# Attention by tiles of 128 tokens, with scores as 64x64 products in the quarters of the array

## The chip, the cores and the metric

The kernel runs on one core of a Trainium2 chip. Its engines are PE (TensorE, matrix products), DVE (VectorE), ACT (ScalarE), POOL (GpSimd) and SP (SyncE, which issues most DMAs). The metric is the time of one execution in device microseconds.

## The reference

Sliding-window attention (4 batches, 8 heads, 576 positions, 64 wide, window 64), whose rows then go through a mixture of 8 experts and a dense two-layer network:

```python
scores = scale * np.matmul(q, k.transpose(0, 1, 3, 2))       # (4, 8, 576, 576), d = 64
mask = (rel >= 0) & (rel < 64)
attn = softmax(np.where(mask, scores, -1e9))
x = (attn @ v).transpose(0, 2, 1, 3).reshape(2304, 512)
...
logits = normed(x) @ normed(expert_emb).T / tau               # one of 8 experts for each token
out[mask] = gate_w[mask, None] * (np.maximum(x[mask] @ w1[e], 0) @ w2[e])
...
h = np.maximum(x @ w_in, 0);  out = (s * h * h + b) @ w_out
```

## The kernel before

The work has three parts: attention with routing, the experts, the dense network. All products are in float32 accuracy. The change is in attention and in the routing of its rows.

A unit is one pair of heads of one batch (16 units); its head pair `hp` puts head `hp` on partitions 0 to 63 and head `hp + 4` on 64 to 127. `prep` (L219) turns a unit's k and q by PE transposes, in four pieces of three transposes and two evictions each. k goes to `kT`, and q into `qbd`, which holds each window of 64 queries as a 128x128 block whose two off-diagonal quarters are zero, cleared once by memsets (`clear`, L179). A batch has nine windows of 64 queries; a window looks at 128 keys.

A step is three windows of one unit, and there are 48 steps in the order of `steps` (L825). In `scores` (L245) one product per window multiplies the block of `qbd` by 128 columns of `kT`: its output has head h's queries in half h of the partitions. It goes to `sp`, one of two buffers in PSUM. DVE then scales, masks and takes the row minimum of the negated scores (L256, one reduction per 128x128 block), POOL subtracts the minimum (L259, steps 2 to 41), ACT takes the exponential (`exps`, L263). `flip` (L272) transposes the blocks on PE and ACT evicts them as `pT`. `pv` (L280) multiplies by v with a column of ones, in half-array products of 64 output rows, into one of two halves of the bank `pob`; DVE normalises into `xs` (L289 to L291). In `xs` partition halves are heads, so a row of the tile is half a token.

When the four units of a window group are through, `fin` (L678) writes `xs` to `x_dram` in two DMAs, sums squares on POOL (`squares`, L399) or with the turn, and plans the routing with `later`: `route_turn` (L376) transposes a window of x, `route_logits` (L393) multiplies it by the expert embeddings (64 output rows, 8 columns), then come rank, count, list, norm and gate for a batch. `route_norm` (L468) adds the two halves' sums of squares with small products against `fold`. The batch that ends at tile `TF` picks the expert that goes first: `first_weights` (L737) loads its weights, which ACT and POOL split in two parts each (`split`, L86).

PE and SP keep the order in which the loop at L875 to L897 issues: pieces of `prep`, scores of step n, flips of step n - lag, what `later` has for step n, then `pv` of step n - lag - 1. The lag is 2 up to step 41 and 1 after it (L845). `prepare` (L869) runs `prep` ahead by `AHEAD` and `RATE`. k and q of the unit after next and v of the next unit are loaded when a unit is prepared (L833 to L836). The other engines are ordered by the planner's priorities.

Of the kernel before, what the change touches and what calls it, by code (L numbers as in the profile page):

```python
# [20 lines left out]
def tile_kernel(ctx, tc, q, k, v, emb, tau, w1, w2, w_in, w_out, s_in, b_in, out, x_dram, y_dram, y0_dram, wi_dram, wo_dram):  # L21
# [15 lines left out]
    TL = 15  # L37
# [113 lines left out]
    npo = [0]  # L151

    def half_bank(n):
        npo[0] += 1
        return pob[:, npo[0] % 2, :n]

# [18 lines left out]
    qbd = [at.tile([128, NW, 2, 64], F32, name=f"qbd{i}") for i in range(NB)]  # L175
# [10 lines left out]
    G = 3  # L186
    PVP = 20
    NG = NW // G
# [15 lines left out]
    mask = at.tile([128, 2, 128], F32, name="mask")  # L204
    nc.gpsimd.memset(mask, 0.0)
    for h in range(2):
        m = mask[64 * h:64 * h + 64]
        nc.gpsimd.affine_select(out=m[:, 0], in_=m[:, 0], compare_op=ALU.is_ge, fill=-8.0e9,
                                base=-1, pattern=[[1, 128]], channel_multiplier=-1)
        nc.gpsimd.affine_select(out=m[:, 0], in_=m[:, 0], compare_op=ALU.is_ge, fill=-8.0e9,  # L210
                                base=64, pattern=[[-1, 128]], channel_multiplier=1)
        nc.gpsimd.affine_select(out=m[:, 1], in_=m[:, 1], compare_op=ALU.is_ge, fill=-8.0e9,
                                base=0, pattern=[[-1, 128]], channel_multiplier=1)

    xs = {}

    ready = {}

    def prep(b, hp):  # L219

        kt, qt = qk.pop((b, hp))
        qd = qbd[(b * NP + hp) % NB]
        kT = kTs[(b * NP + hp) % NB]
        for nm, src in (("k", kt), ("q", qt)):
            for h in range(2):
# [3 lines left out]
                rows = slice(64 * h, 64 * h + 64)  # L229
                for par in range(2):  # L230
                    if nm == "k":
                        o = kT[rows].rearrange("r (c p e) -> r e c p", c=QC, e=2)[:, par]
                        i = pt[64 * par:64 * par + 64]
                    else:
                        o = qd[rows, :, h].rearrange("r (c w) (p e) -> r e c w p", c=QC, e=2)[:, par]
                        i = pt[64 * par:64 * par + 64].rearrange("r c (w p) -> r c w p", p=32)
# [4 lines left out]
                if nm == "q" and h == 1:  # L241
                    ready[b, hp] = qd, kT
                yield

    def scores(b, hp, g):  # L245
        qd, kT = ready[b, hp]
        sp = ps2.tile([128, G, 128], F32, tag="sp", name="sp")
        for i in range(G):
            w = g * G + i
            k0 = max(w - 1, 0) * 64  # L250
            nc.tensor.matmul(sp[:, i], qd[:, w].rearrange("r h c -> r (h c)"), kT[:, k0:k0 + 128], start=True, stop=True)
        sm = at3.tile([128, G, 128], F32, tag="sm", name="sm")
        mn = at3.tile([128, G], F32, tag="mn", name="mn")
        for i in range(G):
            w = g * G + i
            nc.vector.tensor_tensor_reduce(out=sm[:, i], in0=sp[:, i], in1=mask[:, 1 if w == 0 else 0], scale=-1.0 / 8.0,  # L256
                                           scalar=BIG, op0=ALU.add, op1=ALU.min, accum_out=mn[:, i:i + 1])
        if P0 <= now[0] < PS:
            nc.gpsimd.tensor_tensor(sm, sm, mn.unsqueeze(2).to_broadcast([128, G, 128]), op=ALU.subtract)  # L259
            return sm, None  # L260
        return sm, mn

    def exps(sm, mn):  # L263
        pe = at3.tile([128, G, 128], F32, tag="pe", name="pe")
# [3 lines left out]
        for i in range(G):  # L268
            nc.scalar.activation(pe[:, i], sm[:, i], AF.Exp, bias=mn[:, i:i + 1], scale=-1.0)
        return pe  # L270

    def flip(pe):  # L272
        pt = ps1.tile([128, G, 128], F32, tag="pt", name="pt")
        for i in range(G):
            nc.tensor.transpose(pt[:, i], pe[:, i], ident)
        pT = at3.tile([128, G, 128], F32, tag="pT", name="pT")
# [3 lines left out]
    def pv(b, hp, g, pT):  # L280
        po = half_bank(G * (D + 1)).rearrange("p (i d) -> p i d", i=G)
        for i in range(G):
            w = g * G + i
            for h in range(2):
                rows = slice(64 * h, 64 * h + 64)
                nc.tensor.matmul(po[rows, i], pT[:, i, rows], vbufs[(b * NP + hp) % NB][:, vslot(w), h], start=True, stop=True)
        with tc.high_priority(offset=PVP):
            rc = at3.tile([128, G], F32, tag="rc", name="rc")
            nc.vector.tensor_scalar(rc, po[:, :, D], 1e-9, None, op0=ALU.add)  # L289
            nc.vector.reciprocal(rc, rc)  # L290
            nc.vector.tensor_tensor(xs[b][g][:, :, hp], po[:, :, :D], rc.unsqueeze(2).to_broadcast([128, G, D]), op=ALU.mult)  # L291
# [15 lines left out]
    fold = rp.tile([128, 64], F32, name="fold")  # L307
# [370 lines left out]
    def fin(b, hp, g, pT):  # L678
        pv(b, hp, g, pT)
        if hp < NP - 1:  # L680
            return
# [612 lines left out]
```

## Time and profile before

| | us |
|---|---|
| median of 3 runs | 838.13 |
| lowest, highest | 835.36, 838.35 |
| the profiled execution | 838.74 |
| its span | 837.0 |
| PE busy | 800.7 (96%) |
| DVE busy | 525.3 (63%) |
| ACT busy | 391.8 (47%) |
| POOL busy | 250.2 (30%) |

The span is from the first to the last instruction of the profiled execution. A row of busy time gives the union of an engine's instructions; a matmul's end is modelled, so the start-to-start distance in the timeline tells its price and its own length does not. "[0.33 <-DVE xs L291]" behind a row means that the engine stood still for 0.33 us before it and was released by that instruction. Scores start at 8.84 us, the last are at 148.63, and the experts run alone from about 203 us.

### The profile page before, as it was taken

To read this page: it belongs to the slowest core of one execution; us is meant where nothing else is said; L and a number is where in the kernel's file an instruction comes from. 1 tells how busy PE (TensorE), PEld (TensorE's weight loads), DVE (VectorE), ACT (ScalarE), POOL (GpSimd) and SP (SyncE) were. 2 spreads that over 40 slices of the span, in tenths; PEclk is the share of its full clock that TensorE was granted. 3 is DMA by queue.
4 is the path that set the end of the run, shared out by engine and by line. 5 is a ranking of instruction groups with operands and counts; after the bars stand their busy time and mean duration, and the time that the engine had idled before them with its cause. 6 is when DMAs were issued, how large, how long until landed. Compare 5 with 4: busy or idle time off the path is not lost.

```text
span 837.0 us, 16214 instructions
## 1 busy us (share of the span) xinstructions
PE 800.7 (96%) x6078; PEld 741.3 (89%) x6078; DVE 525.3 (63%) x1358; ACT 391.8 (47%) x813; POOL 250.2 (30%) x281
## 2 busy tenths in 40 slices
PE   7999986898999999899899999999999999999996
PEld 6888875798999999899899999999999999999885
DVE  5757987686877668699565555666655444444442
ACT  6968656414534545446354444444535333332331
POOL 7477765260113352444202222222210010101110
PEclk9999998889999999999999999999999999999999
DMA  9988636245749778687463233333324110100000
GB/s 202 216 205 194 137 81 186 94 139 174 245 149 322 232 248 272 210 267 260 163 217 114 101 101 101 107 117 104 115 89 126 52 45 33 51 26 26 26 26 25
DMA packets 103168, 117.12 MB, mean 140 GB/s; under 512 B 39108, under 2 KB 76996, under 8 KB 103088
## 3 DMA queue, kind: packets, MB, share of 16 engines
q1 hardware_dynamic: 93600, 99.11, 40.5%
q0 software_dynamic: 3232, 10.24, 3.5%
q10 hardware_dynamic: 6256, 6.72, 2.4%
q8 instruction: 48, 0.79, 0.4%
q14 instruction: 32, 0.26, 0.1%
HBM read 91.52 MB, written 24.53 MB: 139 GB/s over the span
## 4 chain that ended last, share of the span: by engine, by line
PE 50%; issue 0%; DMA 0%; POOLq 0%; DVE 0%
PE p L126 49%; PE tp L132 1%; DMA out_dram<-o,ids 0%; POOLq L1289 0%; DVE o L1239 0%; POOLq L1240 0%
## 5 line engine op out<-in xcount | busy, mean ns | idle before, releaser
L126 PE MATMUL p<-xl,wh 128*128 128x256 f32 x576 | 162.4, 282 | 0.0
L126 PE MATMUL p<-xh,wh 128*128 128x256 f32 x576 | 162.2, 282 | 0.0
L126 PE MATMUL p<-xh,wl 128*128 128x256 f32 x576 | 161.8, 281 | 0.0
L1201 ACT ACTIVATE r<-p 128x256 f32<-128x256 f32 x144 | 55.2, 384 | 169.6 <-PE p L126 166.2
L1202 DVE SCALAR_TENSOR_TENSOR r<-r,s_bc 128x256 f32<-128x256 f32 x144 | 82.5, 575 | 80.0 <-ACT r L1201 79.7
L1025 POOL TENSOR_TENSOR fl<-fl,fs 128x512 f32<-128x512 f32 x32 | 45.7, 1430 | 251.8 <-DVE fs L1024 218.3
L126 PE MATMUL p<-wh,gh 128*128 128x512 f32 x288 | 113.0, 392 | 0.0
L126 PE MATMUL p<-wl,gh 128*128 128x512 f32 x288 | 113.0, 392 | 0.0
L126 PE MATMUL p<-wh,gl 128*128 128x512 f32 x288 | 113.0, 392 | 0.0
L126 PEld LDWEIGHTS p<-xh,wh 128*128 128x128 f32 x576 | 108.8, 189 | 0.7
L126 PEld LDWEIGHTS p<-xl,wh 128*128 128x128 f32 x576 | 108.6, 189 | 0.8
L126 PEld LDWEIGHTS p<-xh,wl 128*128 128x128 f32 x576 | 109.0, 189 | 0.0
L88 DVE TENSOR_TENSOR wl<-raw,wh 128x1024 fp32r<-128x1024 f32 x72 | 102.4, 1429 | 6.5 <-ACT wh L87 6.3
L87 ACT ACTIVATE wh<-raw 128x1024 fp32r<-128x1024 f32 x80 | 83.3, 1056 | 4.9 <-DMA raw<-wo_dram 2.1
L1240 POOL DMA_INDIRECT out_dram<-o,ids x18 | 18.7, 1040 | 203.8 <-DVE o L1239 183.3
L126 PE MATMUL p<-hh,wh 128*128 128x256 f32 (+5 forms) x256 | 78.7, 307 | 0.0
L126 PE MATMUL p<-hl,wh 128*128 128x256 f32 (+5 forms) x256 | 77.0, 301 | 0.0
L126 PE MATMUL p<-hh,wl 128*128 128x256 f32 (+5 forms) x256 | 76.9, 300 | 0.0
L1208 ACT ACTIVATE gh<-r,b_bc 128x256 fp32r<-128x256 f32 x144 | 72.5, 503 | 6.1 <-DVE r L1202 5.9
L1209 DVE SCALAR_TENSOR_TENSOR gl<-r,b_bc,gh 128x256 fp32r<-128x256 f32 x144 | 69.1, 480 | 3.1 <-ACT gh L1208 3.1
L126 PEld LDWEIGHTS p<-wh,gl 128*128 128x128 f32 x288 | 54.1, 188 | 12.2
L126 PEld LDWEIGHTS p<-wh,gh 128*128 128x128 f32 x288 | 54.1, 188 | 11.4
(240 smaller groups left out, 1595.4 us busy)
## 6 DMA issues: line engine op xcount, KB each, us to landing
raw<-in_moe_w_dram SPq DMA_DIRECT2D x64, 512.0 KB, 4.8
raw<-y_dram SPq DMA_DIRECT2D x18, 512.0 KB, 3.8
vb<-in_v_dram SPq DMA_DIRECT2D x64, 128.0 KB, 3.8
fr<-in_moe_w_in_dram SPq DMA_DIRECT2D x16, 512.0 KB, 5.1
fr<-in_moe_w_out_dram SPq DMA_DIRECT2D x16, 512.0 KB, 4.4
k<-in_k_dram SPq DMA_DIRECT2D x32, 144.0 KB, 4.0
q<-in_q_dram SPq DMA_DIRECT2D x32, 144.0 KB, 3.8
x_dram<-xs SPq DMA_DIRECT2D x24, 192.0 KB, 3.0
```

The costliest lines, as they stand in the source:

```text
L87: a = nc.scalar.activation(hi, src, AF.Copy)
L88: return a.ins, le.tensor_tensor(lo, src, hi.bitcast(F32), op=ALU.subtract).ins
L126: nc.tensor.matmul(ps, a[x], b[y], start=first and j == 0, stop=last and j == 2)
L132: nc.tensor.matmul(ps, x, y, start=j == 0, stop=j == len(k) - 1)
L1025: nc.gpsimd.tensor_tensor(lf, lf, sg.bitcast(F32), op=ALU.mult)
L1201: nc.scalar.activation(r, ps, AF.Relu)
L1202: nc.vector.scalar_tensor_tensor(r, r, s_bc, r, op0=ALU.mult, op1=ALU.mult)
L1208: nc.scalar.activation(gh, r, AF.Identity, bias=b_bc)
L1209: nc.vector.scalar_tensor_tensor(gl, r, b_bc, gh.bitcast(F32), op0=ALU.add, op1=ALU.subtract)
L1240: nc.gpsimd.indirect_dma_start(out=out, out_offset=bass.IndirectOffsetOnAxis(ap=ids[:, k:k + 1], axis=0), in_=o, in_offset=None)
```

## The change

The unit of work in attention becomes a tile of 128 tokens, which is two windows, for one pair of heads. There are 18 tiles. A step holds two such pairs (`slots`): mostly two neighbouring tiles of one head pair, and for the tiles that lie across two batches (4 and 13) one tile with two head pairs. So 36 steps have four blocks of 128x128 scores each where 48 had three.

Each block is made of two products for each head: 64 queries by 128 keys over 64 dimensions. Heads lie in the rows of the array, windows in its columns, so the four products of a slot are in the four quarters. Their output has the 128 tokens on the partitions, with one head per block. The score buffer `spb` is one tile of two banks, a head in each, with both parities of the step in each bank. `qbd` becomes the plain `qTs`, without zeros. `po` is a single buffer. The logits of a tile alternate between the two halves of the columns. `xs` holds whole tokens of 512 values, so the turn takes a tile at a time, the squares need no folding, and x is written with one DMA for one or two tiles.

In a step the flips and the turns come before the scores, the logits and `pv` behind them. The loads of v wait until the buffer is free (`late_v`, `values`). The lag goes to 1 from step 31, the routing batches end after tiles 3, 8, 12 and 15 (`ROUTED`; the second with tile 4), and the last batch has the two tiles 16 and 17 instead of three.

```diff
-    TL = 15
+    TL = 16
...
-    ps2 = ap.enter_context(tc.tile_pool(name="ps2", bufs=2, space=PSUM))
-    pob = ps1.tile([128, 2, 256], F32, tag="po", name="pob")
+    spb = ps1.tile([128, 2, 2, 2, 128], F32, tag="sp", name="spb")
...
-    qbd = [at.tile([128, NW, 2, 64], F32, name=f"qbd{i}") for i in range(NB)]
+    qTs = [at.tile([128, S], F32, name=f"qT{i}") for i in range(NB)]
...
-        en.memset(qbd[i][64:128, :, 0], 0.0)
-        en.memset(qbd[i][0:64, :, 1], 0.0)
         en.memset(vbufs[i][:, :, :, D:], 1.0)
...
+    def unit(t, hp, c):
+        w = 2 * t + c
+        return (w // NW * NP + hp) % NB, w % NW
...
-            nc.tensor.matmul(sp[:, i], qd[:, w].rearrange("r h c -> r (h c)"), kT[:, k0:k0 + 128], start=True, stop=True)
+    def scores(n, slots):
+        for s, (t, hp) in enumerate(slots):
+            for c in range(2):
+                u, i = unit(t, hp, c)
+                k0 = max(i - 1, 0) * 64
+                for h in range(2):
+                    rows = slice(64 * h, 64 * h + 64)
+                    nc.tensor.matmul(spb[64 * c:64 * c + 64, h, n % 2, s], qTs[u][rows, i * 64:i * 64 + 64],
+                                     kTs[u][rows, k0:k0 + 128], start=True, stop=True)
...
+                j = 2 * s + h
+                nc.vector.tensor_tensor_reduce(out=sm[:, j], in0=spb[:, h, n % 2, s], in1=m, scale=-1.0 / 8.0,
+                                               scalar=BIG, op0=ALU.add, op1=ALU.min, accum_out=mn[:, j:j + 1])
...
+        po = ps1.tile([128, 4, D + 1], F32, tag="po", name="po")
+        for s, (t, hp) in enumerate(slots):
             for h in range(2):
+                for c in range(2):
+                    rows = slice(64 * c, 64 * c + 64)
+                    u, i = unit(t, hp, c)
+                    nc.tensor.matmul(po[rows, 2 * s + h], pT[:, 2 * s + h, rows], vbufs[u][:, vslot(i), h], start=True, stop=True)
...
-            add(lg[o:o + 64, w // 2], xt[:, c % 2, c // 2], enT[:, c])
+            for o in range(0, 128, 64):
+                add(lg[o:o + 64, t], xt[:, c, o:o + 64], enT[:, c])
...
-        for o in range(2):
-            add(ssf[64 * o:64 * o + 64, t0:t1], fold, ss[:, 2 * t0 + o:2 * t1:2])
...
+            nc.sync.dma_start(x_dram[t * 128:(t + nt) * 128].rearrange("(s p) n -> p s n", p=128), xs[t])
...
+    ROUTED = {3: ((0, 4), (4, 5, 6, 7, 9, 10, 11, 12, 14)),
+              4: ((4, 9), (3, 4, 5, 6, 7, 8, 9, 10, 12)),
+              12: ((9, 13), (2, 3, 3, 3, 4, 4, 4, 4, 6, 7)),
+              15: ((13, 16), (2, 3, 3, 3, 4))}
...
+    steps = by_pair((0, 2)) + \
+        by_pair((5, 7), (0, 1)) + alone(4, 0) + by_pair((5, 7), (2, 3)) + alone(4, 2) + \
+        by_pair((9, 11)) + alone(13, 0) + alone(13, 2) + by_pair((14,)) + by_pair((16,))
...
+    def values():
+        while late_v and free(late_v[0], nfin[0]):
+            load_v(*units[late_v.pop(0)])
...
-    AHEAD, RATE = 3, 1.9
+    AHEAD, RATE = 3, 2.4
-    P0, PS = 2, 42
+    P0, PS = 2, 31
...
         for n, s in enumerate(steps):
             now[0] = n
             prepare(n)
...
+            flips(n)
+            run(n, HALF)
+            sm, mn = scores(n, s)
...
             pes.append(exps(sm, mn))
-            flips(n)
             run(n)
             fins(n)
+            values()
```

## Rows read from the trace of the kernel before

**Rows 1.** Busy time by stage: length, engines (instructions), clock, DMA share, GB/s.

```profile
core 0: us, PE busy (x) PEld busy (x) DVE busy (x) ACT busy (x) POOL busy (x), PEclk, DMA share, GB/s
28.89:50.00 21.11, 21.08 (x252) 18.50 (x249) 14.51 (x81) 19.35 (x48) 13.58 (x21) 1.00 0.98 223
8.84:107.35 98.51, 95.86 (x1122) 83.92 (x1123) 75.09 (x394) 74.74 (x179) 66.56 (x113) 1.00 0.90 191
107.35:150.07 42.72, 34.20 (x385) 29.25 (x384) 31.89 (x177) 26.32 (x69) 22.91 (x24) 0.90 0.51 147
150.07:203.30 53.23, 46.89 (x426) 45.46 (x426) 38.78 (x128) 18.68 (x39) 18.90 (x13) 0.89 0.38 122
203.30:837.00 633.70, 619.73 (x4132) 579.97 (x4130) 376.17 (x647) 266.82 (x517) 134.23 (x97) 0.99 0.40 133
```

**Rows 2.** Timeline of PE, one step: start, us, engine, line, operation, tiles, shape, count.

```profile
31.09 0.71 PE L228 MATMUL tp<-ident,k 96*128 96x96 f32 x6
31.64 0.86 PE L251 MATMUL sp<-kT,qbd 128*128 128x128 f32 x6
32.33 0.49 PE L275 MATMUL pt<-ident,pe 128*128 128x128 f32 x3
32.81 0.57 PE L286 MATMUL pob<-vb,pT 128*64 128x65 f32 x12
33.31 0.71 PE L228 MATMUL tp<-ident,q 96*128 96x96 f32 x6
```

**Rows 3.** Timeline of PE: logits before full-array transposes, logits before P times V.

```profile
95.96 0.63 PE L319 MATMUL rt<-enT,xt 128*64 128x8 f32 x8
96.53 0.44 PE L381 MATMUL tpx<-ident,xs 128*128 128x128 f32 x2
...
102.40 0.63 PE L319 MATMUL rt<-enT,xt 128*64 128x8 f32 x8
102.83 0.59 PE L286 MATMUL pob<-vb,pT 128*64 128x65 f32 x12
```

**Rows 4.** Groups by form, 8.84 to 107.35: busy us, mean ns | idle before, releaser.

```profile
L256 DVE CUSTOM_DVE_ANT_0 sm<-sp,mask 128x128 f32<-128x128 f32 x108 | 25.7, 287 | 6.4 <-PE sp L251 5.2 <-POOL sm L259 0.4 <-ACT pe L266 0.2
...
L266 ACT ACTIVATE pe<-sm 128x384 f32<-128x384 f32 x33 | 17.2, 522 | 4.1 <-POOL sm L259 3.6
...
L277 ACT ACTIVATE pT<-pt 128x384 f32<-128x384 f32 x34 | 16.5, 486 | 6.5 <-PE pt L275 6.1
...
L291 DVE TENSOR_TENSOR xs<-pob,rc 128x192 f32<-128x192 f32 x32 | 11.4, 356 | 0.9
...
L383 ACT ACTIVATE xt<-tpx 128x256 f32<-128x256 f32 x22 | 8.1, 382 | 5.1 <-PE tpx L381 5.1
```

**Rows 5.** Timeline of PE, then of DVE: two P times V, one normalisation.

```profile
59.64 0.57 PE L286 MATMUL pob<-vb,pT 128*64 128x65 f32 x12 [0.31 <-DVE km L428]
...
62.21 0.57 PE L286 MATMUL pob<-vb,pT 128*64 128x65 f32 x12 [0.33 <-DVE xs L291]
...
61.71 0.36 DVE L291 TENSOR_TENSOR xs<-pob,rc 128x192 f32<-128x192 f32 x1
```

**Rows 6.** DMA from 0 to 60 us; issues of v and k (size, us to landing).

```profile
DMA packets 33798, 12.38 MB, mean 206 GB/s; under 512 B 20229, under 2 KB 33781, under 8 KB 33789
...
vb<-in_v_dram SPq DMA_DIRECT2D x64, 128.0 KB, 3.8
...
k<-in_k_dram SPq DMA_DIRECT2D x32, 144.0 KB, 4.0
```

**Rows 7.** Timeline in the tail: POOL, DVE and PE.

```profile
133.06 9.32 POOL L88 TENSOR_TENSOR wl<-raw,wh 128x1024 fp32r<-128x1024 f32 x4
...
137.89 4.53 DVE L490 TENSOR_SCALAR gt<-gt 128x4 f32<-128x4 f32 x1
...
144.94 0.48 PE L319 MATMUL rt<-Qv,lhot 128*128 128x96 bf16 x4 [4.63 <-DVE Qv L460]
```

**Rows 8.** Timeline of PE: first products of the first expert.

```profile
153.75 0.68 PE L132 MATMUL tp<-xh,wh 128*128 128x208 f32 x4
```

More of the change, by code (lines that the diff above doesn't have):

```diff
@@ L277, in flip, with pv @@
+        for j in range(4):
+            nc.tensor.transpose(pt[:, j], pe[:, j], ident)
+        pT = at3.tile([128, 4, 128], F32, tag="pT", name="pT")
         nc.scalar.activation(pT, pt, AF.Copy)
         return pT
[L280 to L283, printed above, removed]
+    def pv(slots, pT):
+        po = ps1.tile([128, 4, D + 1], F32, tag="po", name="po")
+        for s, (t, hp) in enumerate(slots):
@@ L812, in tile_kernel, with later, run, by_pair @@
     todo = {}
-    def later(n, do):
-        todo.setdefault(n, []).append(do)
-    def run(n):
-        for do in todo.pop(n, []):
-            do()
-    by_pair = [(hp, g) for hp in range(NP) for g in range(NG)]
-    by_win = [(hp, g) for g in range(NG) for hp in range(NP)]
-    mixed = [(hp, g) for p, gs in ((0, (0, 1)), (2, (0, 1)), (0, (2,)), (2, (2,))) for g in gs for hp in (p, p + 1)]
-    ORDERS = (by_pair, mixed, by_win, by_win)
-    steps = [(b, hp, g) for b in range(B) for hp, g in ORDERS[b]]
-    need = [4 * max(b * NP + hp + 1 for b, hp, _ in steps[:n + 1]) for n in range(len(steps))]
+    TURN, WHOLE, HALF, BEHIND = range(4)
+    def later(n, do, kind=WHOLE):
+        todo.setdefault(n, []).append((kind, do))
+    def run(n, end=9):
+        q = todo.get(n, [])
+        for kind in range(end):
+            for k_, do in [x for x in q if x[0] == kind]:
+                q.remove((k_, do))
+                do()
+        if not q:
+            todo.pop(n, None)
+    def by_pair(ts_, hps=range(NP)):
+        return [((t, hp), (t + 1, hp)) for hp in hps for t in ts_]
+    def alone(t, hp):
+        return [((t, hp), (t, hp + 1))]
+    steps = by_pair((0, 2)) + \
+        by_pair((5, 7), (0, 1)) + alone(4, 0) + by_pair((5, 7), (2, 3)) + alone(4, 2) + \
+        by_pair((9, 11)) + alone(13, 0) + alone(13, 2) + by_pair((14,)) + by_pair((16,))
+    FIRST = {t: s[0][0] for s in steps for t, _ in s}
+    used = [[(2 * t + c) // NW * NP + hp for t, hp in s for c in range(2)] for s in steps]
+    need = [4 * (max(u for us in used[:n + 1] for u in us) + 1) for n in range(len(steps))]
+    def free(n, m):
+        return all(n - NB not in us for us in used[m:])
+    late_v = []
+    def values():
+        while late_v and free(late_v[0], nfin[0]):
+            load_v(*units[late_v.pop(0)])
     def preps():
@@ L854, in fins @@
             m = nfin[0]
-            fin(*steps[m], pts[m])
+            assert not late_v or all(u < late_v[0] for u in used[m])
+            fin(steps[m], pts[m])
             nfin[0] += 1
@@ L870, in prepare @@
         want = max(need[m] + (AHEAD if m > n else 0) - RATE * (m - n) for m in range(n, len(steps)))
-        while done[0] < min(want if n else need[0] + 2, 4 * len(units)):
+        while done[0] < min(want if n else need[0] + 2, 4 * len(units)) and free(done[0] // 4, n):
             next(pieces)
             done[0] += 1
+        assert done[0] >= need[n]
     with tc.manual_schedule(engines={mybir.EngineType.PE, mybir.EngineType.SP}):
-        for n, (b, hp, g) in enumerate(steps):
+        for n, s in enumerate(steps):
             now[0] = n
             prepare(n)
-            xs.setdefault(b, {})
-            if g not in xs[b]:
-                end = b == B - 1 and g == NG - 1
-                xs[b][g] = (lp if end else xp).tile([128, G, NP, D], F32, tag="xs", name="xs")
-            sm, mn = scores(b, hp, g)
+            t = s[0][0]
+            if t not in xs:
+                nt = 1 if t == s[1][0] else 2
+                xs[t] = (lp if t == TL else xp).tile([128, nt, DM], F32, tag=f"xs{nt}", name="xs",
+                                                            **({} if t == TL else {"bufs": 2 * nt}))
+                xs[s[1][0]] = xs[t]
+            flips(n)
+            run(n, HALF)
+            sm, mn = scores(n, s)
             if n == 4:
```

219 lines of the change are left out of this document (87 added, 132 removed).

## The prediction

> **What bounds the kernel now.** I read the busy times by stage first [rows 1]. From 203.30 us on, TensorE (PE) is busy 619.7 of 633.7 us at a granted clock of 0.99. The change touches nothing there, so that stretch moves as a block with whatever comes before it. From 8.84 us (first scores) to 107.35 us (36 of 48 steps done, 108 of 144 score blocks) PE is busy 95.9 of 98.5 us, while VectorE (DVE) and ScalarE (ACT) have 75.1 and 74.7: PE sets the pace. From 107.35 to 150.07 us (the last 12 steps) PE has only 34.2 of 42.7 us, at a clock of 0.90, so waits set it. Next I read one step of the PE timeline for the pace of each kind of product [rows 2], and two places for what a change of tiling costs [rows 3]. Last come the waits inside a step [rows 5] and in the tail [rows 7].
>
> **Prices on PE.** A float32 product is two instructions. Six score instructions take 0.69 us (31.64 to 32.33): 0.116 each. Six transposes of `prep` take 0.55 us, 0.092 each; the twelve of P times V take 0.50 us to the next work [rows 2]. Eight logit instructions take 0.43 us where a P times V in the same 128x64 shape follows, so 0.054 each, and 0.57 us where full-array transposes follow [rows 3]: a change of shape costs 0.14 us. Three flips are then 0.48 - 0.14, or 0.11 each, and twelve P times V 0.50 - 0.14, or 0.030 each. The logits of one window go to one half of the columns; P times V alternates halves and runs at nearly half the price. That is the trace's own evidence that neighbours in different parts of the array overlap.
>
> **The sum on PE over all of attention, before.** 48 steps x (6 x 0.116 + 3 x 0.11 + 12 x 0.030 = 1.386) = 66.5; 64 pieces of `prep` (three transposes, 0.275) = 17.6; 36 windows x (2 x 0.11 + 8 x 0.054 = 0.652) = 23.5; changes of shape, two per step and two per window, 168 x 0.14 = 23.5. Together 131 us, against 95.9 + 34.2 busy in the two stretches [rows 1].
>
> **After.** Scores: 16 instructions of 64x64 in each of 36 steps, at a pace p that no row shows. Below, p is a quarter of the full product, 0.029; above, no overlap at all, 0.116 [rows 2]. I take 0.030, the pace of P times V, which is nearest in kind (64 columns of weights, neighbours in other parts). Nothing argues for less than 0.029. Then 36 x (16 x 0.030 + 4 x 0.11 + 16 x 0.030 = 1.40) = 50.4; `prep` 17.6 as before; 18 tiles x (4 x 0.11 + 16 x 0.030 = 0.92, as the logits now alternate halves too) = 16.6; shapes: full to quarters, quarters to halves, halves to full, 3 x 36 x 0.14 = 15.1. Together 99.7 us, 31.5 less: 16.1 from scores, 7.0 from logits, 8.4 from changes of shape. With p = 0.058 (two at a time) it would be 16 less, with 0.116 it would be 18 more.
> A row shows 0.14 us for leaving the half-column shape [rows 3]. The Trainium skill, TensorEngine Tiling (Array Packing), Key Properties, says that a change of tiling mode drains the engine, which speaks against a step with three modes. If entering and leaving the quarters each cost a whole 0.28 us product instead of 0.14, the sum would be 10 us higher, 110; the forecast stays, since PE is no longer the only limit below.
>
> **What catches the saving, first stretch.** Work that filled 36 steps is now in 27. Floors, counted from 8.84 us:
> PE: 27 x (1.40 + 0.42) + 58 pieces x 0.275 + 9 tiles x 0.92 + some 2.5 of ranking = 76 us.
> ACT: 74.7 now [rows 1]. 33 exponentials and 34 evictions of 384 columns (0.52 and 0.49) become 54 of 512. 256 to 384 columns cost 0.10 [rows 4], so about 0.60 each: 32.4 instead of 33.7. 22 turns at 0.38 become 9 at about 0.59: 3 less. Floor 70.
> DVE: 75.1 [rows 1]; the 108 reductions stay (0.24 each), 32 normalisations of 0.36 become some 25 wider ones [rows 4]. Floor 73.
> DMA: k and q of a unit are four transfers of 144 KB, v four of 128 KB [rows 6]. By the 28th step all 16 units of k and q, 12 of v and 9 tiles of x must have moved: 9.4 + 6.3 + 2.4 = 18.1 MB. At 223 GB/s [rows 1] or 206 [rows 6] that is 81 to 88 us from about 2 us on, so 74 to 81 here.
> POOL: 66.6 [rows 1], less fourteen memsets, plus four selects for the mask. No limit; 27 wide subtractions cost about what 36 narrow ones did.
> SP: 16 x writes become six by then; each still stands one step behind its normalisation, and loads queue behind it. The v loads of units 8 to 15 are new in waiting: a unit's buffer is free only after steps 12 or 17 are finished, so they go out at the end of steps 15 to 20 and are first needed three steps after that unit's scores. At 3.8 us a load [rows 6] this is covered unless the loads run at their ceiling, which is what rival (b) prices.
> Four floors lie between 70 and 81, so none hides behind another any more. There is also a new tie. The score buffer is now one tile whose two parities share each bank. The rows show how such a tile behaves: P times V at 62.21 waits for the normalisation of the previous step, ending at 62.07, though it writes the other half of `pob` [rows 5]. So scores of step n will wait for the four reductions of step n-1, where two separate buffers stood before, and behind a waiting score product all of PE's logits, P times V and transposes queue. Scores, reductions and hand-offs are about 0.6 + 1.0 + 0.2 us in a step of 3 us: covered as long as DVE is not late by over a microsecond; it costs that lateness if it is. Making `po` single costs nothing, since its halves behave as one already [rows 5]. The flips now stand ahead of the scores; two steps of lag, 6 us, cover the chain of reduction, subtraction and exponential (some 3 us) here, but not in the tail. I take 1.07 times the highest floor: 86 us or 3.2 a step, 12 less than 98.5 (bounds 78 to 97).
>
> **Second stretch.** 36 blocks remain, now 9 steps. The first four at 3.2 us are 12.8. In the last five the lag is one step and the flips of step n-1 stand ahead of the scores of step n, so scores 0.6, reductions 1.0, an exponential 0.5, flips 0.6 and hand-offs 0.3 are in series, 3.0, and 3.3 with the turns: 16.5. A hole remains: DVE's `gt` instruction takes 4.53 us from 137.89 and ends with POOL's four weight splits at 142.4, and PE idles 4.63 us to 144.94 [rows 7]. The Trainium skill, SBUF: State Buffer, Who interferes with whom, calls the port that DVE shares with POOL an exclusive lock, and the trace agrees. Splits and gates stay near each other in the new order, so I leave the hole in; without it the time would be 4.6 lower. Sum 33.9 against 42.7: 9 less (0 to 14).
>
> **Third stretch.** 53.2 us to 203.30 [rows 1]; the last batch has two tiles instead of three, the norms lose their fold products, x is written in whole rows. I cost these at nothing: the loads and the first expert set this stretch. That cover could fail at one place, the weights of the first expert: their splits end at 142.4 [rows 7] and are first used at 153.75 [rows 8], 11.4 us spare. The batch that picks that expert now ends 10 steps (some 40 us) before the end of attention, where it was 12 steps (some 45): 5 of the 11.4 are used up, none is exceeded.
>
> **Sum.** The profiled execution took 838.74 us, 0.6 above the median of 838.13. 838.7 - 12 - 9 = 818 us.
>
> **Rivals.**
> (a) Everything keeps up with PE, as DVE and ACT did at 0.76 of their time [rows 1], and the 31.5 us pass through: 807. Against it: the floors.
> (b) The bank tie and the loads bind: 3.5 us a step in the first stretch (95, gain 4), 4.1 a step later (37, gain 6): 829. For it: DMA already moves 191 GB/s over that stretch [rows 1], and DVE's lateness shows at 62.21 [rows 5].
> (c) The same but with steps of 3.65 and 4.7 us (98.5 and 42.3): 838. Then PE's free time is only new idle time.
> (d) Slower: the quarters don't overlap, so the change doesn't do what its words say. Each step pays 16 x 0.086 = 1.4 us more, 49.5 in all, 18 more than is saved: 857. It decides from p = 0.085, where the sums are equal. Against it: P times V's 0.030.
> (e) Slower: PE, no longer busy, loses its clock. It was 0.90 in the stretch where PE was busy 80% of the time, 1.00 where it was 97% [rows 1]. At 0.75 in the first stretch PE's 76 us become 101, 3 more than now, and the tail gains nothing: 842 to 845.
>
> **How the numbers follow.** A measurement of this kernel can tell about 0.5%, 4 us. Chances: forecast (811 to 826) 0.52, (a) 0.10, (b) 0.13, (c) 0.12, (d) 0.06, (e) 0.07. Faster is forecast, (a) and (b): 0.75; same is (c): 0.12; slower is (d) and (e): 0.13. The range keeps (a), the forecast, (b) and the near half of (c): 805 to 838. What it leaves out is (d), (e) and the far half of (c), 0.19.
>
> **What will show it.** Score instructions at 0.03 us start to start, in a step 0.5 instead of 0.9 us per four blocks; the 28th step at about 95 us; last scores near 129; the same 633.7 us behind. PE's busy share in the first stretch falls to some 0.88, with waits on `sm` reductions and loads. Wrong: p over 0.085 (d), a clock under 0.9 there (e), scores that wait for DVE by over 0.5 us a step (b, c), or first-expert products that wait for their splits, which would give the tail's gain back.

## The result and the profile after

| | before | after |
|---|---|---|
| median, us | 836.75 | 846.98 |
| lowest, highest | 835.23, 838.35 | 844.96, 851.04 |
| profiled execution, its span | 838.74, 837.0 | 851.04, 849.2 |

The ratio is 1.0128 (95% interval 1.0083 to 1.0173): slower by 1.3%, where 818 us was forecast. The profiled execution after is the slowest of its four, so its stages show some 12 us where the medians show 10. The stages of the kernel after follow, cut at the same events as [rows 1] (first scores, 108 of 144 blocks done, end of attention, experts alone). Columns: stretch, length, busy time of each engine (instructions), granted clock of PE, DMA share, GB/s.

```profile
core 0: us, PE busy (x) PEld busy (x) DVE busy (x) ACT busy (x) POOL busy (x), PEclk, DMA share, GB/s
8.33:112.81 104.48, 87.56 (x1304) 70.46 (x1304) 68.44 (x374) 72.50 (x157) 55.56 (x84) 0.90 0.80 182
112.81:153.40 40.59, 31.23 (x463) 24.88 (x460) 30.40 (x151) 24.72 (x51) 24.03 (x22) 0.81 0.46 161
153.40:213.50 60.10, 48.01 (x439) 47.04 (x436) 39.64 (x129) 18.05 (x36) 18.09 (x13) 0.82 0.30 96
213.50:849.00 635.50, 619.47 (x4138) 579.33 (x4136) 376.67 (x649) 267.05 (x517) 134.26 (x97) 0.99 0.40 133
```

Against [rows 1] the first stretch is 6.0 us longer, the second 2.1 shorter, the third 6.9 longer; behind it the time is the same within 2. PE's work did fall (95.86 to 87.56 busy in the first stretch), but its idle time there rose from 2.6 to 16.9 us, and its clock left 1.00. Of that idle time the three largest groups, and the wait of scores for reductions, are (us in total, times, longest):

```profile
PE po L280 <- DVE xs L289: 3.5, 2, 2.7
PE pt L268 <- ACT pT L270: 3.1, 4, 1.0
PE tp L224 <- DMA k<-in_k_dram: 2.0, 1, 2.0
PE spb L241 <- DVE mn L249: 1.4, 4, 0.5
```

So scores waited 1.4 us in 27 steps for the reductions of the step before, and PE 2.0 us for a load. One step of PE, in columns as in [rows 2]:

```profile
35.67 0.67 PE L241 MATMUL spb<-kT,qT 64*64 64x128 f32 x16
36.26 0.69 PE L280 MATMUL po<-vb,pT 128*64 128x65 f32 x16
36.88 0.47 PE L224 MATMUL tp<-ident,q 96*128 96x96 f32 x3
```

Sixteen score instructions take 0.59 us to the next work, change of shape included, where six took 0.69 for three blocks [rows 2]. The quarters overlap.

Three waits show where the time may go. First, 60 to 72 us: DVE works off the ranking of the first tiles, and P times V waits for a normalisation behind it (PE, DVE, POOL).

```profile
64.24 0.67 PE L241 MATMUL spb<-kT,qT 64*64 64x128 f32 x16 [0.43 <-DVE mn L249]
67.64 1.14 PE L280 MATMUL po<-vb,pT 128*64 128x65 f32 x16 [2.74 <-DVE xs L289]
68.71 1.12 PE L268 MATMUL pt<-ident,pe 128*128 128x128 f32 x4
...
64.39 1.02 DVE L442 TENSOR_TENSOR kj<-kt,iota 128x16 f32<-128x16 f32 x1
...
67.07 0.42 DVE L289 TENSOR_TENSOR xs<-po,rc 128x256 f32<-128x256 f32 x1
...
64.33 1.05 POOL L252 TENSOR_TENSOR sm<-sm,mn 128x512 f32<-128x512 f32 x1 [2.54 <-DVE gt L478]
```

PE stands 2.74 us, and at 68.71 four flips last 1.12 us where they last 0.66 at 37.55: half clock (the granted clock is 0.50 from 67 to 72 us). Second, SP's queue, and PE behind it:

```profile
83.61 8.50 SPq L185 DMA_DIRECT2D vb<-in_v_dram  x12
92.15 1.27 SPq L159 DMA_DIRECT2D k<-in_k_dram  x2
...
96.78 1.38 PE L224 MATMUL tp<-ident,k 96*128 96x96 f32 x6 [2.04 <-DMA k<-in_k_dram]
```

Three units' v loads become free at once and go out ahead of the next k. Third, behind attention (POOL, DVE, PE):

```profile
165.90 9.30 POOL L88 TENSOR_TENSOR wl<-raw,wh 128x1024 fp32r<-128x1024 f32 x4
...
165.95 2.35 DVE L467 TENSOR_SCALAR nrm<-nrm 128x5 f32<-128x5 f32 x1 [1.38 <-POOL nrm L460]
168.34 0.19 DVE L468 RECIPROCAL nrm<-nrm 128x5 f32<-128x5 f32 x1
168.44 0.13 DVE L412 COPY logit<-rt 128x16 f32<-128x16 f32 x1
168.61 0.17 DVE L413 TENSOR_REDUCE mxs<-logit 128x2 f32<-128x16 f32 x1
168.70 1.97 DVE L471 TENSOR_TENSOR L<-logit,nrm 128x40 f32<-128x40 f32 x1
170.59 2.35 DVE L416 TENSOR_TENSOR eq<-logit,mxs 128x16 f32<-128x16 f32 x1
172.97 2.26 DVE L418 TENSOR_TENSOR eq<-eq,w 128x16 f32<-128x16 f32 x1
...
175.47 0.17 DVE L420 TENSOR_TENSOR oh<-w,km 128x16 bf16<-128x16 f32 x1
...
175.70 0.17 PE L316 MATMUL rt<-oh,tri 128*128 128x16 bf16 x1 [7.67 <-DVE oh L420]
```

Four DVE instructions of the last ranking and gate, each worth some 0.2 us, end only when one of POOL's four weight splits ends, and PE stands 7.67 us. In the kernel before, two splits came ahead of the norm and two behind it, and PE stood 2.48 us (POOL, PE):

```profile
161.17 4.74 POOL L88 TENSOR_TENSOR wl<-raw,wh 128x1024 fp32r<-128x1024 f32 x2 [18.79 <-ACT wh L87]
165.86 1.20 POOL L472 TENSOR_TENSOR nrm<-nrm,half 128x5 f32<-128x5 f32 x1
...
166.44 0.18 PE L319 MATMUL rt<-oh,tri 128*128 128x24 bf16 x1 [2.48 <-DVE oh L429]
```

From the last scores to expert 0's first product of 256 columns it is 47.95 us here (152.32 to 200.27), 38.92 before (148.63 to 187.55): this is the largest single loss, 9.0 us. Up to the last ranking's product (`rt<-oh,tri`) it is 23.4 us instead of 17.8, behind it 24.6 instead of 21.1.

### The profile page after: what moved, and what is told of

Its sections match the earlier page's. It is cut to its first block, busy times and chain, and to the rows that moved or that the text cites. A ratio compares the mean times of both kernels' runs of the same rounds, so it can differ in the third digit from the quotient of the medians.

```text
span 849.2 us, 16607 instructions
## 1 busy us (share of the span) xinstructions
PE 790.2 (93%) x6350; PEld 724.4 (85%) x6350; DVE 516.7 (61%) x1310; ACT 387.1 (46%) x770; POOL 237.2 (28%) x248
## 5 line engine op out<-in xcount | busy, mean ns | idle before, releaser
L1214 DVE SCALAR_TENSOR_TENSOR r<-r,s_bc 128x256 f32<-128x256 f32 x144 | 79.9, 558 | 78.0 <-ACT r L1213 77.6
L1221 DVE SCALAR_TENSOR_TENSOR gl<-r,b_bc,gh 128x256 fp32r<-128x256 f32 x144 | 71.2, 495 | 3.1 <-ACT gh L1220 3.1
L132 PE MATMUL tp<-xh,wh 128*128 128x256 f32 (+6 forms) x288 | 55.9, 319 | 12.2 <-DVE hl L749 5.5
## 6 DMA issues: line engine op xcount, KB each, us to landing
k<-in_k_dram SPq DMA_DIRECT2D x32, 144.0 KB, 3.5
q<-in_q_dram SPq DMA_DIRECT2D x32, 144.0 KB, 3.4
```

What stands on the lines that cost most here:

```text
L132: nc.tensor.matmul(ps, x, y, start=j == 0, stop=j == len(k) - 1)
L1214: nc.vector.scalar_tensor_tensor(r, r, s_bc, r, op0=ALU.mult, op1=ALU.mult)
L1221: nc.vector.scalar_tensor_tensor(gl, r, b_bc, gh.bitcast(F32), op0=ALU.add, op1=ALU.subtract)
```

## The experiments

The expectations name theories, in the order in which they were formed: at first that hand-offs set the pace and PE no longer does; A, that the tie of the score banks does; B, that DVE's bursts of ranking do; C, a serial chain through all engines; D, bursts of preparation; E, PE with its holes and the half clock behind them. A hole is a wait of PE, half clock a granted clock of 0.50.

"The 28th step" is counted from the first scores; 104.48 us in the kernel after. Two runs further down leave PE's and DVE's order up to there untouched (e3_both 104.95, j1_fill 103.66), so about 1 us is not to be read.

**Which engine's amount of work sets the first stretch?** Each score product twice (e1_twice), half of the reductions twice (d2_dve), q copies moved from DVE to ACT (e2_qact), POOL's subtraction moved into ACT's exponentials (h1_nosub), half of the score products (l1_half; the rest of its score buffer is cleared once).

```diff
 e1   for _ in range(2): nc.tensor.matmul(spb[...], ...)
 d2   for _ in range(2 if s == 0 else 1): tensor_tensor_reduce(out=sm[:, j], ...)
 e2  -TOACT = (("k", 0), ("k", 1))
     +TOACT = (("k", 0), ("k", 1), ("q", 0), ("q", 1))
 h1  -if P0 <= n < PS:
     +if False:
 l1  -for s, (t, hp) in enumerate(slots):
     +for s, (t, hp) in enumerate(slots[:1]):
```

> The changed kernel with each 64x64 score product issued twice (the same numbers are written over themselves), so PE carries 16 more instructions of about 0.03 us in each of 36 steps: 17 us more, 13 of them in the first 27 steps. Theory (PE no longer sets the pace; hand-offs among DVE, ACT and POOL do): at most a third of it shows, 849 to 853 us against the changed kernel's 847. Rival (PE at a falling clock is still the bound): most of it shows, 859 to 865.

> The changed kernel with two of the four reductions of each step done twice (the same numbers again), 0.43 us more of DVE in each of 36 steps, 15.5 us in all, 11.6 of them in the first 27 steps. Doubling the score products on PE, 0.48 us a step, showed in full. Theory C (one serial chain through the engines): these 0.43 us show in full too, 860 to 866. Rival (PE alone is the bound and DVE, busy 68 of 104 us, has slack): at most a third shows, 847 to 852.

> The changed kernel with both halves of every q copy on ACT, as the k copies are, so that DVE never stands on a q copy until ACT has let go of the same bank. ACT carries 32 more copies of about 0.43 us, 14 us. Theory (DVE, in order, standing behind ACT's half: 20.6 us of waits in the first stretch): the first stretch is 4 to 8 us shorter, 839 to 843 us. Rival (the wait is only a symptom, DVE would wait elsewhere, or ACT is the pace): no change or a loss, 846 to 855.

> The changed kernel without the subtraction on POOL: the row minimum goes into the exponential as a bias, four ACT instructions of 128 columns a step instead of one of 512, as the last steps do it. POOL loses 28 instructions of 1.04 us and no longer stands in the path from scores to flips; ACT gains about 0.4 us a step, 11 us in all. Theory C (a step is a chain through DVE, POOL, ACT and back to PE, with two steps of lag, and DVE's ranking instructions stand still for the 1 us of a subtraction): the first 27 steps 4 to 10 us shorter, 837 to 843. Rival (ACT is as near to its limit as the others): 847 to 856.

> The changed kernel with half of the score products left out (eight of the sixteen of each step; the other half of the scores stays at zero, so the attention of those blocks is wrong and the tokens go to other experts: only the time up to the last scores is to be read). PE has 0.24 us less a step, 6.5 us in the first 27 steps. Theory E (PE and its holes set the pace, so each us of PE counts, as the doubled products seemed to show): the 28th step 5 to 7 us sooner than in the changed kernel, 97.5 to 99.5 us after the first scores. Rival (below the present amount of PE work the hand-offs set the pace): 102 to 105, as with the whole products (102.2 to 105.4).

Medians and ratios to the kernel before: e1 868.76 us, 1.0375 (1.0352 to 1.0397); d2 856.62, 1.0201 (1.0160 to 1.0242); e2 852.39, 1.0201 (1.0168 to 1.0235); h1 845.17, 1.0084 (1.0055 to 1.0114). The whole time of l1, 878.76 us (1.0499), says nothing here, since its tokens go to other experts. The first 27 steps, columns as above. Scores twice (e1_twice):

```profile
8.48:127.34 118.86, 100.88 (x1736) 84.12 (x1735) 71.38 (x382) 72.47 (x157) 54.47 (x84) 0.91 0.69 160
```

Reductions twice (d2_dve):

```profile
8.30:114.10 105.80, 86.64 (x1304) 69.40 (x1304) 83.50 (x486) 72.72 (x158) 55.09 (x83) 0.92 0.78 180
```

q copies on ACT (e2_qact):

```profile
8.35:114.79 106.44, 86.58 (x1304) 69.05 (x1303) 55.36 (x344) 87.36 (x189) 55.38 (x84) 0.90 0.78 179
```

No subtraction on POOL (h1_nosub):

```profile
8.39:113.78 105.39, 84.44 (x1304) 66.89 (x1304) 66.46 (x383) 88.93 (x233) 29.90 (x59) 0.94 0.79 180
```

Half of the scores (l1_half, cut 0.17 us ahead of the 28th step):

```profile
8.41:112.00 103.59, 87.47 (x1088) 67.58 (x1087) 71.50 (x379) 72.19 (x157) 55.49 (x84) 0.85 0.81 184
```

DVE 15.1 us busier: 1.3 longer. ACT 14.9 busier and DVE 13.1 less: 2.0 longer. ACT 16.4 busier and POOL 25.7 less: 0.9 longer. So neither the amount of DVE's, of ACT's nor of POOL's work sets this stretch. Doubling the scores added 13.3 us to PE and 14.4 to the stretch, which looked as if PE set it. Halving them doesn't fit that: with 6.5 us less work the 28th step came at 103.8, 0.7 sooner, which is not to be read. PE's busy time stayed at 87.47, since its clock fell to 0.85: some 31 us of half clock instead of 21, which would cost a PE at its limit 5 us. So the clock may have eaten most of the saving. Against that stands only that half clock looks cheap in this stretch where three kernels are compared (behind the filler run below); the two are not separated by a run. Nor does the doubling show evenly: by the 13th step it had cost 2.2 of its 5.8 us (43.68 against 41.51). The present amount of PE's work seems to lie near a bend: more of it costs, less brings little. The rest of d2's loss is in the steps with a lag of one: its last scores start 155.2 us after the first, where the kernel after has 144.0.

**The tie of the score banks.** One score buffer in the kernel before (b1_tie); in the changed kernel, all turns (q, k, x, flips) in two PSUM buffers instead of three and one (f2_ctl), and the two banks so freed given to the scores, odd and even steps apart (f2_notie).

```diff
 b1  -ps2 = ... name="ps2", bufs=2, ...
     +ps2 = ... name="ps2", bufs=1, ...
 f2  -ps3 ... bufs=3        -pt = ps1.tile(..., tag="pt")
     +ps3 ... bufs=2        +pt = ps3.tile(..., tag="tp")
 f2_notie also
     -spb = ps1.tile([128, 2, 2, 2, 128], ...)
     +spbs = [ps1.tile([128, 2, 4, 128], ...) for i in range(2)]
```

> The kernel before with one score buffer in place of two, so that the six score products of a step wait for the three reductions of the step before: the new tie alone, without the change. Theory A (the tie closes a loop of scores and reductions, which is why PE's work shows in full): 6 us or more slower than the kernel before, 842 to 853 us. Theory B (the time goes where DVE is filled by ranking work, and in the half clock after each hole of PE; the tie matters little): 835 to 840.

> The changed kernel with two buffers of PSUM, instead of three and one, for all turns (q, k, x and the flips). It gives up two of the eight banks, and is the base for the next kernel, where the two banks go to the scores. Cost of having fewer buffers for turns: 0 to 15 us over the changed kernel, 847 to 862.

> As the kernel with two buffers for all turns, and with the scores of odd and even steps in banks of their own (four banks), so that scores don't wait for the reductions of the step before. Compared with that base: Theory A (the tie sets the pace of the first stretch): 6 to 15 us faster than the base. Theory B (ranking bursts and the clock): within 3 us of the base.

b1: 841.3 us, 1.0039 (1.0017 to 1.0062), and its first stretch:

```profile
8.95:111.58 102.63, 98.59 (x1122) 85.03 (x1123) 76.47 (x394) 75.66 (x179) 66.90 (x114) 1.00 0.85 183
```

The tie costs 4.1 us over these 36 steps of the kernel before (98.51 to 102.63 [rows 1]), 3 in the medians. It is real and too small: Theory A falls by its own bound of 6. f2_ctl took 901.02 us, 1.0776 (1.0721 to 1.0832), and f2_notie 903.45, 1.0772 (1.0731 to 1.0813): without the tie nothing is gained on that base. (Both f2 kernels also give the first expert's output one buffer instead of two, behind this stretch.) The surprise is the base itself, far outside the 0 to 15 us expected. The first 27 steps of f2_ctl:

```profile
11.07:158.18 147.11, 112.30 (x1305) 86.21 (x1304) 70.06 (x377) 74.41 (x156) 54.08 (x81) 0.78 0.53 126
```

The weight loads of its flips in this stretch, as a group (busy us, mean ns | idle before them, releasers):

```profile
L268 PEld LDWEIGHTS pt<-ident,pe 128*128 128x128 f32 x104 | 15.6, 185 | 27.4 <-ACT kT L229 16.5 <-DVE qT L231 10.7
```

The stretch is 42.6 us longer: 17.9 of it are idle time of PE, 24.7 busy time, at a clock of 0.78 and with half pace at the start (last section). The flips' weight loads alone waited 27.4 us, almost all for copies of k and q out of the two buffers. No engine's amount of work moved it nearly as much as the number of PSUM buffers between PE and the engines that empty them.

**The order inside a step, the lag, the spread of preparation, ranking.** Scores ahead of the flips, as before (e4_order); three steps from scores to flips (h2_lag3); preparation from earlier on (h3_rate); all of DVE's order written by hand (g1_hand); only the ranking kept from moving forward (i2_spread).

```diff
 e4  -flips(n); run(n, HALF); scores; exps; run(n)
     +scores; exps; flips(n); run(n)
 h2  -return 2 if m < PS else 1
     +return 3 if m < 18 else 2 if m < PS else 1     (pe: bufs=4)
 h3  -AHEAD, RATE = 3, 2.4
     +AHEAD, RATE = 3, 1.9
 g1  +manual_schedule(engines={PE, SP, DVE}); fins(n) ahead of ranking
 i2  +with tc.issue_after(red[0].ins): do()
```

> The changed kernel with the old order on PE inside a step: scores first, then the turns of the flips, of x and the logits, which is how the kernel before had it. Theory (the order on PE doesn't set the pace of the first stretch): within 3 us of 847. Rival (flips standing ahead of the scores hold DVE's reductions back): 838 to 842, with the first 27 steps 5 us or more shorter.

> The changed kernel with three steps instead of two between scores and flips in the first 18 steps (one more buffer for the exponentials). Theory C (the chain from scores to flips is longer than two of the shortened steps): the first 18 steps, 76.24 - 8.33 us in the changed kernel, are 4 to 8 us shorter, 839 to 843. Rival (what binds lies inside one step: PE products, P times V waiting for normalisations, turns waiting for copies): within 3 us of 847.

> The changed kernel with the preparation of q and k spread as in the kernel before (1.9 pieces a step at most counted backward instead of 2.4), so it starts earlier and runs less in bursts. Theory D (steps with many pieces are held by PE and ACT, steps with ranking by DVE, and the sum of these maxima is the time): 2 to 6 us faster than the changed kernel, 841 to 845. Rival (the pieces' place doesn't matter): within 2 us of 847.

> The changed kernel with DVE's order in attention written out by hand, as PE's is: q copies, four reductions, then the normalisation of P times V, and the ranking of finished tiles only behind these. Theory B (DVE's ranking instructions stand ahead of normalisations, and P times V waits for these since it has one buffer): the first 27 steps are 4 to 8 us shorter and the waits of 2 to 3 us of PE at 67 us and the like go; 838 to 843. Rival (any fixed order of DVE stalls as much in other places): 846 to 855.

> The changed kernel where the instructions of ranking and gating stay behind the reductions of the step for which they were written, on DVE: the planner had moved gate instructions of the first batch some five steps forward, into the same two steps as its list instructions (60 to 72 us). Theory E with the ranking bursts as one source of holes: the hole of 2.74 us at 67.64 and the half clock from 66.0 to 73.0 go, 4 to 6 us sooner at the 19th step, 841 to 843. Rival (DVE has slack there: 15 us more of reductions cost the first stretch 1 us): within 3 us of 847.

| run | median, us | ratio (interval) | the 28th step, us |
|---|---|---|---|
| e4_order | 862.87 | 1.0300 (1.0253 to 1.0348) | 117.1 |
| h2_lag3 | 869.33 | 1.0360 (1.0320 to 1.0401) | 119.4 |
| h3_rate | 870.00 | 1.0370 (1.0331 to 1.0410) | 124.4 |
| g1_hand | 878.79 | 1.0479 (1.0442 to 1.0517) | 116.5 |
| i2_spread | 859.23 | 1.0254 (1.0216 to 1.0292) | 104.9 |

All worse, and all slower than either theory expected. The waits named here cover only part of each loss. In e4 PE's busy time rises to 96.6 us (one change of shape more in a step, about 27 x 0.14 = 3.8 of the 9), and its idle time to 20.5. In h2 the 19th step comes 3 us later, not sooner: the chain from scores to flips doesn't set the pace (Theory C falls). In h3 the pieces are asked for before their loads land, 5.6 us of PE waits on k loads by 29 us. In g1 one wait for the router's set-up takes 7.5 us. In i2 the hole of 2.74 us gives way to two of 1.3 and 1.4, the stretch is as long as it was, and from there to the last scores it takes 9.8 us more: the ranking burst by itself isn't the cause either, and ranking pushed back lands where the lag is one step.

**Two single causes, and the clock.** At most one unit's late v loads at a time (i1_vload); 56 transposes that nobody reads, in PE's hole up to 175.70 (j1_fill); the first expert's low halves split by DVE (e3_both).

```diff
 i1  -while late_v and free(late_v[0], nfin[0]):
     +if late_v and free(late_v[0], nfin[0]):
 j1  +for j in range(56): nc.tensor.transpose(fl[:, j % ND], ident, ident)
      route_count(TL, NTT)
 e3  -hl, do = load_part(srcs[c], nc.gpsimd)      (both places)
     +hl, do = load_part(srcs[c], nc.vector)
```

> The changed kernel with the late v loads issued for at most one unit at a time: in the changed kernel twelve v loads take SP's queue 8.50 us from 83.61 us on, and the k loads behind them go out at 92.15, so that PE stands 2.04 us at 96.78 and its clock is at half from 97.0 to 103.5. Nothing else in the order of any engine changes. Theory E (PE still sets the pace, but each hole costs itself and the half clock behind it): the hole and this half clock go, the 28th step starts 4 to 6 us sooner, 841 to 843 us. Rival (the time lies in a chain through the other engines, and a hole of PE is only where it shows): less than 2 us sooner, 845 to 848.

> The changed kernel with 56 transposes of the unit matrix, which nobody reads, on PE at the place of its longest hole (7.67 us, up to 175.70 us, where it waits for the last ranking), about 6.2 us of work that ends before the hole does. Theory E (the clock is at half from 172.0 to 182.0 because of the hole): the half clock behind the hole is gone or shorter, and expert 0's first product comes 2 to 4 us sooner, 843 to 845. Rival (the clock falls for another reason, or PE's work there is not what sets the end): no change or the filler's own excess, 847 to 850.

> The changed kernel with the eight low halves of the first expert's weight splits on DVE (1.22 us each where DVE does it elsewhere) instead of POOL (2.36 each, during which DVE instructions stand still). Theory (in the third stretch the last ranking runs behind four POOL splits, in the second one gate instruction does): the first product of expert 0 comes 5 to 9 us sooner after the last scores, and one PE hole of 3.1 us goes: 837 to 842 us. Rival (the third stretch is a chain of ranking instructions that is as long without the splits): 845 to 848.

i1: 850.45 us, 1.0152 (1.0106 to 1.0199), no gain that the whole time can show. The 28th step is at 102.23, 1.4 to 2.7 us sooner than in the three runs with the old queue: the hole of 2.04 and the half clock at 97 are gone, and another, smaller one has come. That lies between Theory E's 4 to 6 and its rival's under 2.

j1: 850.24 us, 1.0169 (1.0113 to 1.0225): the whole time shows no gain. The same 10 us by engine, in the kernel after:

```profile
172.00:182.00 10.00, 6.30 (x32) 6.30 (x32) 6.88 (x26) 1.15 (x4) 3.20 (x2) 0.50 0.01 2
```

With the filler (j1_fill):

```profile
172.00:182.00 10.00, 7.96 (x73) 7.69 (x72) 9.50 (x30) 1.50 (x5) 3.81 (x2) 1.00 0.00 0
```

The half clock is gone from these 10 us, and the way from the last scores to expert 0's first product is 47.0 us instead of 47.95; behind the last ranking's product alone it is 23.0 (176.64 to 199.60) instead of 24.6. So with the hole filled the clock did not fall, and the 10 us of half clock had cost 1 to 1.6 us here. In the first stretch the comparison is weaker: j1 has some 14 us of half clock there, the kernel after and e3_both some 20, with the same order of instructions; the 28th step comes 0.8 to 1.3 us sooner, where a PE at its limit would have gained 3. That is one profile of each.

e3: 843.25 us, 1.0079 (1.0057 to 1.0101), some 4 us less than the kernel after, at intervals that overlap. From the last scores to expert 0's first product it is 40.72 us (154.21 to 194.93), 7.2 less. Up to the last ranking's product it is 17.7, level with the 17.8 before the change. The ranking still stands behind four DVE splits, and PE behind it:

```profile
171.95 0.17 PE L316 MATMUL rt<-oh,tri 128*128 128x16 bf16 x1 [4.01 <-DVE oh L420]
```

What follows the ranking is another matter. h1_nosub keeps POOL's four splits, and PE stands even longer behind them:

```profile
171.54 0.17 PE L316 MATMUL rt<-oh,tri 128*128 128x16 bf16 x1 [8.01 <-DVE oh L420]
```

Yet from there to expert 0's first product (192.02) it takes 20.5 us, where the kernel after takes 24.6, e3 23.0, i1 25.9 (173.54 to 199.48) and the kernel before 21.1. The half clock is worth 1.6 us of that spread (j1); the rest is open.

**Together.** DVE splits, the second set of them only behind the last ranking's list, the last gate behind that ranking, v loads one unit at a time (k1_tail); the same and the exponentials of h1 (k2_tail_nosub).

```diff
+ranked = route_rank(TL, NTT).ins
 route_count(TL, NTT); route_list(TL, NTT); qv = part(TL, NTT, 0, 2)
+with tc.issue_after(parted[0].ins):
+    for do in dos: do()
 ...
+with tc.issue_after(ranked):
     route_gate(TF, NTT)
```

> The changed kernel with the first expert's low halves on DVE, the second half of them only behind the last ranking's list (in the run with all low halves on DVE, PE stood 4.0 us at 171.95 behind four splits), the last gate behind that ranking, and the late v loads one unit at a time. Theory (third stretch: the last ranking waits for splits): 3 us better than the run with the low halves on DVE, whose hole was of 4.0, and up to 2 from the v loads: 838 to 841. Rival (another link of the chain is as late): 842 to 845.

> As the kernel before this one, and the row minima as biases of four exponentials in place of POOL's subtraction, which by itself gained 2 us (the first stretch was 1 longer, the others shorter). If the gains add up: 836 to 839, level with the kernel before the change. If they were the same gain twice: 838 to 842.

k1: 839.96 us, 1.0032 (1.0012 to 1.0051); k2: 839.59, 1.0023 (1.0005 to 1.0042). Neither beats the kernel before; they take back 8 to 9 of the 10.7 us that the change lost (1.0128). The stretches of k1, cut at the 28th step, the last score product and expert 0's first product:

```profile
8.43:110.24 101.81, 84.77 (x1305) 68.03 (x1304) 68.28 (x374) 72.46 (x157) 55.22 (x84) 0.93 0.79 187
110.24:152.08 41.84, 29.33 (x461) 23.57 (x458) 31.57 (x153) 27.01 (x54) 14.70 (x18) 0.84 0.45 156
152.08:189.01 36.93, 31.00 (x357) 28.85 (x350) 27.34 (x118) 9.39 (x24) 9.18 (x9) 1.00 0.31 105
```

The third stretch is now 37.3 us from the last scores (151.68 to 189.01), shorter than the 38.92 before, and PE's clock in it is 1.00. The second is as long as before the change (41.4 us from the 28th step to the last scores, 41.3 before), and the first still 3.3 us longer.

## Why the prediction was wrong

**PE's sum: right.** p was put at 0.030; 0.59 us for 16 instructions and one change of shape of some 0.14 leave 0.028. The floor of 76 us for the first 27 steps: 87.56 busy, and a mean clock of 0.90 over 104.48 us accounts for at most 10.4 of it, which leaves 77; the half pace of the first 10 us, which the clock column doesn't show (last section), takes off some 4 more. Rival (d) is out.

**"1.07 times the highest floor": the step that failed**, 86 us against 104.48. It took the stretch to run at the largest of four sums of work, with 10 us above PE's own. What the kernel after shows in its place is 16.9 us of idle PE and a clock of 0.90. And the runs show that a sum of work is not what it runs at: 6.5 us less on PE, or 13 less on DVE with as much more on ACT, shorten it by 1 or not at all; 15 us more on DVE or ACT lengthen it by 1 to 2. (For PE the clock is mixed in, as said at l1_half.) That steps of 3.9 us are what hand-offs between in-order engines through single or few buffers take is what remains; it is argued, not shown. Of the 18.5 us missed, the runs place 1.4 to 2.7 (v loads). The tie took 4.1 in the kernel before; in the changed one it was only tried on the base with two turn buffers, where it took nothing. The remaining 12 to 17 are open. The buffers for turns are the one resource that moved the stretch strongly, but only in taking them away; giving more was not tried: the kernel's tiles already take eight banks (two for scores, three and one for turns, one each for `po` and `rt`). The largest single group of PE's waits, 3.5 us, is at the single `po`, which the prediction had put at nothing; whether a second one would have saved them was not tried either.

**The tie: rightly named, its price right in kind.** "Covered as long as DVE is not late by over a microsecond" allowed a few us, and b1_tie measured 4.1. Rival (b) made it the cause; in the changed kernel PE's scores waited 1.4 us for reductions in 27 steps, where its sign was 0.5 a step.

**The v loads: half seen.** The text asked when v is needed, and found it covered; what stands behind a v load in SP's queue is a k load, and that was not. It cost 1.4 to 2.7 us up to the 28th step; the whole time of i1_vload shows no gain.

**The second stretch:** 40.59 against 33.9. Its series of 3.0 us a step left out four waits of PE, of 1.3 to 3.1 us, at a clock of 0.81; the two longest, and what DVE stood behind at the second:

```profile
129.93 0.55 PE L375 MATMUL tpx<-ident,xs 128*128 128x128 f32 x3 [2.74 <-DVE xs L289]
...
150.06 1.21 PE L268 MATMUL pt<-ident,pe 128*128 128x128 f32 x4 [3.12 <-ACT pe L262]
...
146.24 2.41 DVE L502 TENSOR_TENSOR go<-li 128x2 f32<-128x2 f32 x1
...
139.29 9.33 POOL L88 TENSOR_TENSOR wl<-raw,wh 128x1024 fp32r<-128x1024 f32 x4
```

At the second, a gate instruction of DVE ends only with POOL's splits (148.62), and the reductions of the last step but one, their exponentials and PE's flips follow it: the hole that the prediction had left in.

**The third stretch, "costed at nothing": wrong by 6.9 us**, 9.0 up to expert 0's first product. The text asked whether the weights come too late for the experts and found 6 us to spare. What counted was what POOL's splits hold up: in the new order the gate's norm and all four splits came ahead of the last ranking. e3_both takes POOL's splits away and with them the 5.6 us up to the ranking's product; k1_tail's whole way is shorter than before the change. The other 3.5 us, behind the ranking, vary between kernels and stay open. The Trainium skill, SBUF — State Buffer, Who interferes with whom, which the prediction cited for the hole behind 137.89, says that a DVE instruction with two SBUF inputs contends with a POOL instruction that reads SBUF, and the trace agrees (2.35 and 2.26 us for L416 and L418, 0.13 for a copy out of PSUM shortly before them). The prediction applied it to the one hole that the kernel before showed, not to the instructions that the change moves next to the splits.

**Rival (e)** came nearest to the time (842 to 845), with a clock of 0.75 in the first stretch, where it was 0.90, and a tail that gains nothing, where it lost. That it came so near is luck. The clock did fall behind holes, but in the third stretch j1_fill took 10 us of half clock away and gained 1; what half clock cost the first stretch is not settled.

## What to carry to other kernels

Work taken off the bounding engine need not come back as time (here PE's busy time fell by 8.3 us and the stretch grew by 6.0): halve and double that work, and compare what each does to the time, with the granted clock beside it. For a stretch costed at nothing, list which instructions the change puts next to long POOL instructions and which loads it puts behind which in one queue; the two losses that could be taken back here, in whole or in part, were of that kind. Before you put a loss down to half clock, fill the hole ahead of it and see whether the end moves.

## What the runs showed of the hardware

What stands behind a POOL split is not every DVE instruction: with four splits from 165.90 to 175.2 in the kernel after, tensor-tensor and tensor-scalar instructions took 1.97 to 2.35 us, while a reciprocal, a copy out of PSUM and a reduction between them took 0.13 to 0.19. Nor is it one split for each: in j1_fill the instruction L471 stood behind three in a row, and the ranking that followed was quick but no sooner.

```profile
169.23 6.64 DVE L471 TENSOR_TENSOR L<-logit,nrm 128x40 f32<-128x40 f32 x1
```

PE starts at half pace here while the clock column reads 1.00. Two steps at the start of the kernel after, in the timeline of PE:

```profile
15.88 1.13 PE L241 MATMUL spb<-kT,qT 64*64 64x128 f32 x16
18.88 0.67 PE L241 MATMUL spb<-kT,qT 64*64 64x128 f32 x16 [0.15 <-DVE mn L249]
```

The window around the first of them, by engine:

```profile
8.00:18.00 10.00, 8.88 (x77) 6.66 (x76) 5.27 (x26) 7.43 (x21) 0.70 (x3) 1.00 1.14 226
```

With two turn buffers (f2_ctl) sixteen scores still take 1.13 us at 33.88, and 0.67 from 38.28 on. For the first steps the pace of the rows tells more than that column.
